# Pooled attention and a tanh-shrink layer on one core: the output product of the last three groups as seven products of quarters

## The chip, the core and the metric

The kernel runs on one core of one Trainium2 chip. The core has five engines, each with its own instruction queue: TensorE (PE in the profile, with its weight loads as PEld), VectorE (DVE), ScalarE (ACT), GpSimd (POOL) and SyncE (SP), which here only issues DMA transfers. TensorE writes its results to PSUM, a memory of eight banks with 512 f32 columns in 128 partitions each; VectorE and ScalarE read them from there into SBUF, GpSimd works on SBUF alone.

The metric is the device time of one execution in microseconds, as the median of several runs.

## What is computed

Pooled attention over 8 batches, 8 heads, 576 queries of 64 elements: keys and values are averaged over 8 neighbouring positions (576 become 72), and each query attends to the 72 pooled positions. The result, 4608 tokens of 512 elements, goes through a layer that widens it to 2048, applies h - tanh(h) and narrows it to 512.

```python
k_p = k.reshape(B, H, Sp, pool, D).mean(axis=3)
v_p = v.reshape(B, H, Sp, pool, D).mean(axis=3)
scores = scale * np.matmul(q, k_p.transpose(0, 1, 3, 2))
scores = scores - np.max(scores, axis=-1, keepdims=True)
attn = np.exp(scores)
attn = attn / (np.sum(attn, axis=-1, keepdims=True) + 1e-09)
attn_out = np.matmul(attn, v_p)                       # 8 x 8 x 576 x 64
x = attn_out.transpose(0, 2, 1, 3).reshape(B * S, H * D)
h = x @ w_in                                          # 4608 x 2048
g = h - np.tanh(h)
out = g @ w_out                                       # 4608 x 512
```

## The kernel before

**Groups.** The 4608 tokens are worked in nine groups of 512. Groups 0 to 7 hold the first 512 tokens of batches 0 to 7, as four blocks of 128; group 8 holds the tails, the last 64 tokens of every batch. Group 0 is written out by hand together with the start of the kernel; groups 1 to 8 run in one loop (`for g in range(1, NG)`, line 706).

**One group** has two phases on TensorE.

- The h phase: 16 steps `i`, each a `h_mms` of four matmuls of 512 columns (line 386) that gives 128 of the 2048 hidden elements in one PSUM bank. After every second step `h_act` works on two banks at once: ScalarE's Tanh into `t_sb` (line 399), then VectorE's subtraction into `gT`, 128 x 1024 in bf16 (line 400). The steps take banks 0 to 5 in turn, so a pair of banks is written again three pairs later.
- The output product: for each of four token blocks `tb`, 16 matmuls of 512 columns (`o_mms`, line 429), four to a unit `u`, 16 units in all. `gT` holds the weights of the array, `w2b` streams through. A finished block is copied by ScalarE to `o_sb` (line 450) and stored by SP (line 453). In group 8 the last block goes through `o_last`: first 384 columns, then 128, each with its copy and its stores.

**The next batch's attention** is laid into the phases of the group before by a table written out by hand, `plan`. Its keys are places: negative ones stand in the h phase (-16 is the first step), the others are units of the output product. Its entries are steps:

- `("s", n)`: the score matmuls of block n (`s_mms`, line 275), then on VectorE the maximum (line 287) and the subtraction (line 290), `s_shift`.
- `("e", n)`: ScalarE's Exp into `E` (line 303).
- `("t", n)`: SP's DMA transpose of two blocks of `E` into `ET` (line 312).
- `("a", n)`: the value matmuls (`av_mms`, line 339), then VectorE's reciprocal and product (`normalise`, lines 360 and 361).
- `("x", n)`: SP's DMA transpose of two normalised blocks into `xT` (line 369), from which the next group's h phase reads.

Block 4 of some batches is the tails' block: two batches' 64 remaining queries together, for group 8. Batch 7 and the last tail's block are worked during group 6. Groups 7 and 8 have nothing of the kind beside them.

**Engines beside.** GpSimd pools values and keys (`pool_v`, lines 208 to 220, and `pool_k`, lines 193 to 199), up to batch 7's values in group 6; ScalarE casts queries (line 244). The order of each engine's queue is the order in which the program is written; an instruction that waits holds up what is behind it on its engine.

Of the kernel before, what the change touches and what calls it, by code (L numbers as in the profile page):

```python
# [28 lines left out]
NK = H * G  # L29
KP = 2 * G  # L30
D1 = D + 1
SCALE = 1.0 / (POOL * float(D) ** 0.5)


@with_exitstack
def kernel(
# [16 lines left out]
    opool = ctx.enter_context(tc.tile_pool(name="opool", bufs=4))  # L53
# [7 lines left out]
    def two(banks, n):  # L61
# [32 lines left out]
    v_sm = const.tile([128, NT, 1, D], FP32, name="v_sm")  # L94
    x_tl = const.tile([128, 1, 2, 4, D], BF16, name="x_tl")
    warm = const.tile([128, 1], FP32, name="warm")
    v_bf = [
        v_raw[i]
        .rearrange("p t n -> p (t n)")
# [1 line left out]
        .rearrange("p (t n) -> p t n", t=NT)  # L101
        for i in range(2)
    ]

    def xT_of(g):
        return xTs[g % 2] if g < B else xTt
# [176 lines left out]
    def s_shift(banks):  # L283
# [8 lines left out]
        )  # L292
        return sh


    def slot(n):
        return E_ps[n // 2 % 2], ET_ps[n // 2 % 2], n % 2
# [129 lines left out]
    def o_mms(tb, i0, i1, bank, c0=0, c1=DM):  # L427
        for i in range(i0, i1):
            nc.tensor.matmul(  # L429
                PS[:, bank, 0 : c1 - c0],  # L430
                lhsT=gT[:, i, tb * 128 : (tb + 1) * 128],
                rhs=w2b[:, i, c0:c1],
                start=(i == 0),
                stop=(i == NHID - 1),
            )
# [10 lines left out]
    stores = []  # L446

    def o_store(g, tb, bank, eng):
        o_sb = opool.tile([128, DM], FP32, name="o_sb", tag="o_sb")
# [6 lines left out]
    def o_last(g, tb, banks):  # L456
        o_sb = opool.tile([128, DM], FP32, name="o_sb", tag="o_sb")
        for n, (c0, c1, eng) in enumerate(
            ((0, 384, nc.scalar.copy), (384, DM, nc.vector.tensor_copy))
        ):  # L460
            o_mms(tb, 0, NHID, banks[n], c0, c1)
            eng(out=o_sb[:, c0:c1], in_=PS[:, banks[n], 0 : c1 - c0])
            for s, (r0, r1, dst) in enumerate(out_rows(g, tb)):
                (nc.sync, nc.scalar)[s].dma_start(out=dst[:, c0:c1], in_=o_sb[r0:r1, c0:c1])

    def fill(n, bank, cols=512):
        for _ in range(n):
# [237 lines left out]
    hn = [0]  # L705
    for g in range(1, NG):
        nb = g + 1 if g + 1 < B else None
        more = nb is not None and nb + 1 < B

        tail = {2: 0, 3: 1, 5: 2, 7: 3}.get(nb)  # L710
        plan = {}
        if nb is not None:
            units = [(s_block(nb, j), av_block(nb), slot(4 * nb + j)) for j in range(4)]
            s_pairs, a_pairs = [0, 0, 0, 1, 2], [0, 1, 0, 2, 1]
            plan = {
                -12: [("s", 0)],
                -9: [("e", 0)],
                -8: [("s", 1)],
                -5: [("e", 1), ("t", 0)],
                -3: [("s", 2)],  # L720
                0: [("e", 2)],
                1: [("s", 3)],
                3: [("e", 3), ("t", 1)],
                4: [("a", 0)],
                5: [("a", 1), ("x", 0)],
                9: [("a", 2), ("a", 3), ("x", 1)],
            }
            if g == 1:
                plan[-10], plan[-7], plan[-5] = plan.pop(-12), plan.pop(-9), plan.pop(-8)
                plan[-2], plan[-1] = [("e", 1), ("t", 0)], plan.pop(-3)  # L730
            if tail is not None:
                units.append((s_tail(tail), av_tail(tail), slot_tl))
                plan[3].append(("s", 4))
                plan[4] += [("e", 4), ("t", 2)]
                if g == 1:
                    plan[6], plan[7] = plan[4][:1], plan.pop(5)
                    plan[4] = plan[4][1:]
                    plan[10] = plan.pop(9)
                plan[12] = [("a", 4), ("x", 2)]
            xs = [x_pair(), x_pair(), x_tl]  # L740
        if nb is not None:
            pool_v(nb, nc.gpsimd)
        shs = {}

        def step(kind, n):
# [9 lines left out]
            if kind == "s":  # L755
                bk = PAIRS[s_pairs[n]]
                s_mms(s, bk)
                shs[n] = s_shift(bk)
            elif kind == "e":
                s_exp(shs[n], sl)  # L760
            else:
                bk = PAIRS[a_pairs[n]]
# [11 lines left out]
        for u, (tb, qd) in enumerate(UNITS):  # L774
            if g == NG - 1 and tb == 3:
                o_last(g, tb, (0, 1))
                break
# [22 lines left out]
_INS = ['q', 'k', 'v', 'moe_w_in', 'moe_w_out']  # L800
# [26 lines left out]
```

## Time and profile before

Three runs: 307.48 us in the median, 306.88 to 308.18. The profiled execution took 306.89 us, of which its span, from the first to the last instruction, is 305.1 us. The mean granted TensorE clock is 0.994 of full speed.

| stage (us from the span's start) | length | TensorE | VectorE | ScalarE | GpSimd | DMA share |
|---|---|---|---|---|---|---|
| group 5, h phase (184.98 to 198.80) | 13.82 | 13.82 | 9.89 | 9.01 | 7.67 | 0.84 |
| group 5, output product (198.80 to 215.03) | 16.23 | 16.12 | 8.62 | 5.77 | 6.23 | 0.86 |
| group 6, h phase (215.03 to 229.43) | 14.40 | 14.40 | 10.47 | 8.90 | 7.60 | 0.46 |
| group 6, output product (229.43 to 246.16) | 16.73 | 16.57 | 10.20 | 4.72 | 0.13 | 0.57 |
| group 7, h phase | 13.81 | 13.81 | 7.81 | 7.76 | 0.00 | 0.08 |
| group 7, output product | 13.82 | 13.71 | 1.98 | 2.78 | 0.00 | 0.16 |
| group 8, h phase (273.79 to 287.60) | 13.81 | 13.81 | 7.82 | 7.76 | 0.00 | 0.05 |
| group 8, output product and end (287.60 to 305.10) | 17.50 | 13.96 | 2.27 | 3.26 | 0.00 | 0.27 |

The table gives busy time in us. TensorE's share is close to the length of each stage, while the other engines have room, most of it in groups 7 and 8; group 6's VectorE has least. A stage of group 6 is longer than one of group 7 by the matmuls of batch 7's attention that stand between the product's own.

Three things help in reading the lines further on. A group's row gives the source line, the engine, the operation, output and inputs with partitions x elements, the count, the busy time and the mean of one, then the engine's idle time before them and what ended it. A row of the timeline gives the start, the length and what ran. Matmuls are pipelined: the record of one is longer than the distance to the next.

### The profile page before, as it was taken

Reading aid. Unit: us, or ns where it says so; the run is one execution under the profiler, and the core shown is the slowest. Engines: PE = TensorE matmul, PEld = TensorE weight load, DVE = VectorE, ACT = ScalarE, POOL = GpSimd, SP = SyncE. Lnnn points to the kernel's source line nnn. Section 1 sums busy time; section 2 is a strip of 40 time slices with the busy share of each in tenths; the row PEclk is TensorE's granted clock in tenths of the full one; section 3 lists DMA queues with packets and bytes.
Section 4 is the critical chain, followed back from the end, with each engine's and each line's share of the span. In section 5 each row is a group of like instructions: output and inputs, shape, how many; then the busy total and the mean of one; then the engine's idle time right before and its main releaser. Section 6 shows DMA issues by size and latency. Waiting matters only on the chain.

```text
span 305.1 us, 4524 instructions
## 1 busy us (share of the span) xinstructions
PE 290.4 (95%) x1734; PEld 150.4 (49%) x1757; DVE 179.4 (59%) x250; ACT 142.3 (47%) x186; POOL 113.5 (37%) x101
## 2 busy tenths in 40 slices
PE   5779989899999999999999999999999999999995
PEld 1457955444554455445544554455445544444443
DVE  4696766458844993398249933983399336305700
ACT  2467756157504751476147613761474136225511
POOL 7544929209610791097109710971080000000000
PEclk9799999999999999999999999999999999999999
DMA  7999997898999998876898799879803830020023
GB/s 232 220 223 309 217 281 164 157 269 288 198 219 213 345 161 183 284 261 123 200 275 280 142 165 282 289 91 219 252 15 73 183 94 0 9 97 34 0 63 77
DMA packets 85894, 54.84 MB, mean 180 GB/s; under 512 B 60368, under 2 KB 73040, under 8 KB 85872
## 3 DMA queue, kind: packets, MB, share of 16 engines
q1 hardware_dynamic: 78192, 44.84, 58.7%
q0 software_dynamic: 6400, 8.91, 14.2%
q10 hardware_dynamic: 1280, 0.79, 0.9%
q8 instruction: 14, 0.23, 0.3%
q14 instruction: 8, 0.07, 0.1%
HBM read 36.70 MB, written 9.44 MB: 151 GB/s over the span
## 4 chain that ended last, share of the span: by engine, by line
PE 84%; DVE 5%; DMA 4%; ACT 4%; issue 1%; ACTq 0%; DVEq 0%
PE PS L429 38%; PE PS L386 35%; PE PS L339 4%; PE PS L275 3%; PE PS L408 2%; DMA k_raw<-in_k_dram 2%; DMA xT<-x_sb 2%; PE PS L256 1%; ACT E L303 1%; DVE sh L290 1%; DVE mx L287 1%; DVE gT L421 1%; DVE x_sb L361 1%; ACT qT L521 1%; ACT t_sb L420 1%
## 5 line engine op out<-in xcount | busy, mean ns | idle before, releaser
L429 PE MATMUL PS<-w2b,gT 128*128 128x512 bf16 (+2 forms) x570 | 131.4, 373 | 1.4 <-ACT v_sm L651 0.2
L400 DVE TENSOR_TENSOR gT<-PS,t_sb 128x1024 bf16<-128x1024 f32 x64 | 77.2, 1220 | 63.4 <-ACT t_sb L399 63.4
L386 PE MATMUL PS<-xT,w1b 128*128 128x512 bf16 x448 | 100.6, 379 | 1.1 <-DMA xT<-x_sb 1.1
L399 ACT ACTIVATE t_sb<-PS 128x1024 f32<-128x1024 f32 x64 | 65.6, 1024 | 44.5 <-PE PS L386 44.5
L429 PEld LDWEIGHTS <-gT 128*128 128x128 bf16 x592 | 54.8, 98 | 58.5 <-issue 0.5
L386 PEld LDWEIGHTS <-w1b 128*128 128x128 bf16 x512 | 49.3, 98 | 58.0 <-issue 2.3
L450 ACT COPY o_sb<-PS 128x512 f32<-128x512 f32 x33 | 19.3, 584 | 73.6 <-PE PS L429 73.6
L208 POOL TENSOR_TENSOR v_raw<-v_raw 128x1280 f32<-128x1280 f32 x6 | 17.4, 2906 | 40.7 <-DMA v_raw<-in_v_dram 40.7
L303 ACT ACTIVATE E<-sh 128x576 bf16<-128x576 f32 x32 | 21.8, 681 | 19.8 <-DVE sh L290 19.8
L287 DVE TENSOR_REDUCE mx<-PS 128x8 f32<-128x576 f32 x36 | 26.9, 748 | 5.6 <-PE PS L275 5.6
L290 DVE TENSOR_TENSOR sh<-PS,mx 128x576 f32<-128x576 f32 x36 | 27.3, 757 | 1.2
L360 DVE RECIPROCAL rden<-PS 128x8 f32<-128x8 f32 x36 | 7.3, 204 | 27.5 <-PE PS L339 27.4
L361 DVE TENSOR_TENSOR x_sb<-PS,rden 128x512 bf16<-128x512 f32 x32 | 22.1, 691 | 1.1
L193 POOL TENSOR_TENSOR k_raw<-k_raw 128x1280 f32<-128x1280 f32 x7 | 20.3, 2905 | 0.1
L244 ACT CAST q_bf<-q_raw 128x1024 bf16<-128x1024 f32 x14 | 14.4, 1038 | 5.5 <-DMA q_raw<-in_q_dram 5.5
L339 PEld LDWEIGHTS <-ET 128*128 128x128 bf16 x192 | 13.1, 98 | 6.1 <-ACT ET L322 0.8
L230 POOL COPY KB<-kT 64x288 bf16<-64x288 bf16 x12 | 5.1, 421 | 29.5 <-DMA kT<-kd 17.8
L408 PE MATMUL PS<-xT,w1b 128*128 128x256 bf16 x128 | 15.3, 273 | 0.7 <-ACT xT L378 0.7
L339 PE MATMUL PS<-VB,ET 128*128 128x130 bf16 (+2 forms) x192 | 15.7, 221 | 0.2 <-ACT ET L322 0.2
L275 PE MATMUL PS<-KB,qT 128*128 128x144 bf16 x128 | 13.1, 226 | 1.3 <-ACT KB L230 0.9
L275 PEld LDWEIGHTS <-qT 128*128 128x128 bf16 x128 | 9.9, 98 | 8.8 <-issue 1.6
L386 PE MATMUL PS<-xTt,w1b 128*128 128x512 bf16 x64 | 14.0, 379 | 0.0
(75 smaller groups left out, 171.7 us busy)
## 6 DMA issues: line engine op xcount, KB each, us to landing
out_dram<-o_sb SPq DMA_DIRECT2D x32, 256.0 KB, 2.7
k_raw<-in_k_dram SPq DMA_DIRECT2D x14, 512.0 KB, 8.4
v_raw<-in_v_dram SPq DMA_DIRECT2D x12, 512.0 KB, 5.0
q_raw<-in_q_dram SPq DMA_DIRECT2D x11, 512.0 KB, 6.8
w1b<-in_moe_w_in_dram POOLq DMA_DIRECT2D x4, 512.0 KB, 9.0
q_raw<-in_q_dram POOLq DMA_DIRECT2D x2, 1024.0 KB, 15.1
w2b<-in_moe_w_out_dram POOLq DMA_DIRECT2D x4, 512.0 KB, 19.2
v_raw<-in_v_dram POOLq DMA_DIRECT2D x2, 512.0 KB, 13.7
```

Source lines behind the costliest of these rows:

```text
L193: eng.tensor_tensor(out=r[:, :, 0:4, :], in0=r[:, :, 0:4, :], in1=r[:, :, 4:8, :], op=ALU.add)
L275: nc.tensor.matmul(PS[ps, banks[m // 2], KP * (m % 2) : KP * (m % 2) + KP], lhsT=qT[:, m, :], rhs=KB[kb][:, m, :], start=True, stop=True,)
L287: nc.vector.reduce_max(out=mx.rearrange("p k h o -> p k (h o)"), in_=sc, axis=AX.X)
L290: nc.vector.tensor_tensor(out=sh[:, :, :, :], in0=sc, in1=mx.to_broadcast([128, 2, 4, G]), op=ALU.subtract)
L303: nc.scalar.activation(out=E[:, e, :, :].rearrange("p t c -> p (t c)")[:, 0:NK], in_=sh.rearrange("p k h c -> p (k h c)"), func=ACT.Exp, s ...
L339: nc.tensor.matmul(PS[ps, banks[half], D1 * h : D1 * (h + s1 - s0)], lhsT=ET[:, t, c0 : c0 + (ps.stop - ps.start)], rhs=VB[kb][:, t, s0:s1 ...
L361: nc.vector.tensor_tensor(out=x_sb, in0=ps[:, :, :, 0:D], in1=rden.to_broadcast([128, 2, 4, D]), op=ALU.mult,)
L386: nc.tensor.matmul(PS[:, bank, :].rearrange("p (j c) -> p j c", j=R), lhsT=w1b[:, fb, i * 128 : (i + 1) * 128], rhs=xT_of(g)[:, :, fb, :], ...
L399: nc.scalar.activation(out=t_sb[:, :, :], in_=ps, func=ACT.Tanh)
L400: nc.vector.tensor_sub(out=gT[:, i : i + 2, :], in0=ps, in1=t_sb[:, :, :])
L408: h_mm_last[0] = nc.tensor.matmul(PS[:, bank, 256 * s : 256 * s + 256].rearrange("p (j c) -> p j c", j=2), lhsT=w1b[:, fb, (2 * n + s) * 1 ...
L429: nc.tensor.matmul(PS[:, bank, 0 : c1 - c0], lhsT=gT[:, i, tb * 128 : (tb + 1) * 128], rhs=w2b[:, i, c0:c1], start=(i == 0), stop=(i == NH ...
```

## The change

**Seven products.** In groups 6, 7 and 8 (`SEVEN`) the output product is taken apart. The 512 x 2048 matrix of a group's `gT` and the 2048 x 512 of `w2b` are cut in halves in both directions, and the product of quarters, which takes eight products of 256 x 1024 by 1024 x 256, is formed from seven, with sums of quarters as their factors (the scheme of Strassen in Winograd's form). Each product has two halves of 128 tokens (`b`), and each of those eight matmuls of 256 columns.

- Four sums of `w2b`, T1 to T4, each in two halves of 128 x 1024 in bf16, are formed once by VectorE in the output product of group 5, one at each unit from 8 on. They lie in the buffers of raw keys and values.
- Four sums of `gT` for each group, S1 to S4, lie in the buffers of raw queries. S3 is formed in two halves (128 x 1024) behind the last two `h_act`, S2 (128 x 2048) at u = 2 and S4 (128 x 2048) at u = 8, all on VectorE; S1 in two halves on GpSimd, behind S2.
- The products run in the order 4, 2, 7, 1, 6, 5, 3. Product 2 has bank 2; the others are added up one after the other in banks 0 and 1, one for each `b`, and each intermediate state that an output needs is copied out before the next product goes on in that bank. In group 6, ScalarE copies and GpSimd forms the differences with earlier states; in groups 7 and 8 VectorE subtracts while it copies.
- Output goes to two fixed tiles `o_h` (`o_hs`), half a group each, in all groups. In groups 6 to 8 it is stored in halves, in group 8 the first half in two pieces of 256 columns.

```diff
+    LO, HI = slice(0, NQ), slice(NQ, NHID)
+    C1, C2 = slice(0, HC), slice(HC, DM)
+    def w_sums():
+        b11, b12, b21, b22 = ((HI, C1), (HI, C2), (LO, C1), (LO, C2))
+        w = lambda q: w2b[:, q[0], q[1]]
+        ops = [
+            (T1, w(b12), w(b11)),
+            (T2, w(b22), T1),
+            (T3, w(b22), w(b12)),
+            (T4, w(b21), T2),
+        ]
...
+    def g_sum(n, i0, i1, eng=nc.vector):
+        i = slice(i0, i1)
+        a11, a12 = gT[:, NQ + i0 : NQ + i1, C1], gT[:, i, C1]
+        a21, a22 = gT[:, NQ + i0 : NQ + i1, C2], gT[:, i, C2]
+        o, x, y, op = {
+            1: (S1, a21, a22, ALU.add),
+            2: (S2, a22, S3[:, i, :], ALU.subtract),
+            3: (S3, a11, a21, ALU.subtract),
+            4: (S4, a12, S2[:, i, :], ALU.subtract),
+        }[n]
+        return eng.tensor_tensor(out=o[:, i, :], in0=x, in1=y, op=op)
+    XB, YB = 2, (0, 1)
+    PRODUCTS = ("4", "2", "7", "1", "6", "5", "3")
+    def product(n, b):
+        A, a0, B_ = {
+            "1": (gT[:, HI, C1], 0, w2b[:, HI, C1]),
+            "2": (gT[:, LO, C1], 0, w2b[:, LO, C1]),
+            "3": (S4, 0, w2b[:, LO, C2]),
+            "4": (gT[:, LO, C2], 0, T4),
+            "5": (S1, 0, T1),
+            "6": (S2, 0, T2),
+            "7": (S3, 0, T3),
+        }[n]
+        ps = PS[:, XB, HC * b : HC * b + HC] if n == "2" else PS[:, YB[b], 0:HC]
+        for i in range(NQ):
+            nc.tensor.matmul(
+                ps,
+                lhsT=A[:, i, 128 * b : 128 * b + 128],
+                rhs=B_[:, i, :],
+                start=(n in "24" and i == 0),
+                stop=(i == NQ - 1),
+                skip_group_check=True,
+            )
+    def evacuate(n, b, plain=False):
+        ps = PS[:, YB[b], 0:HC]
+        if n == "2":
+            if b == 1:
+                nc.scalar.copy(out=p2, in_=PS[:, XB, :].rearrange("p (b c) -> p b c", b=2))
+        elif n in "47":
+            nc.scalar.copy(out={"4": n0, "7": n1}[n][:, b, :], in_=ps)
+        elif n == "6":
+            nc.scalar.copy(out=o_hs[1][:, b, C1], in_=ps)
+        elif plain and n in "15":
+            dst = o_hs[0][:, b, C1] if n == "1" else o_hs[1][:, b, C2]
+            nc.scalar.copy(out=dst, in_=ps)
+        else:
...
+            nc.vector.tensor_sub(out=dst, in0=ps, in1=sub[:, b, :])
...
+        for u in range(14 if g in SEVEN else 0):
+            n, b = PRODUCTS[u // 2], u % 2
+            product(n, b)
+            evacuate(n, b, nb is not None)
+            for it in plan.get(u, ()):
+                step(*it)
+                run_late()
+            if u == 2:
+                dep = g_sum(2, 0, NQ)
+                after([g_sum(1, 0, 4, nc.gpsimd), g_sum(1, 4, NQ, nc.gpsimd)], dep)
+            if u == 8:
+                g_sum(4, 0, NQ)
+            if b == 0:
+                continue
+            if n == "1":
+                finish_11(nc.gpsimd, nb is not None)
+                if g == NG - 1:
+                    store_half(g, 0, C1)
+            elif g == NG - 1 and n == "5":
+                store_half(g, 1)
+            elif g == NG - 1 and n == "3":
+                store_half(g, 0, C2, (nc.sync, nc.scalar))
+            elif n in "53":
+                if n == "5" and nb is not None:
+                    finish_22(nc.gpsimd)
+                store_half(g, 0 if n == "3" else 1)
```

**The order around it.** The h phase of groups 6 to 8 takes its banks in another order, so that the last pair lies in banks 4 and 5. Group 6 has its own plan: all four score blocks of batch 7 stand in the h phase, the fourth (`"sb"`) before the last `h_act`, and the value blocks at u = 3, 5, 6 and 7 of 14. The tail's scores come at u = 9; its value matmuls, their normalisation and their transpose are carried into group 7's h phase, at steps 3 and 5.

```diff
+    HB = ((2, 3), (4, 5), (0, 1))
+    PLAN7 = {
+        -14: [("s", 0)],
+        -11: [("e", 0)],
+        -10: [("s", 1)],
+        -7: [("e", 1), ("t", 0)],
+        -6: [("s", 2)],
+        -3: [("e", 2)],
+        -1: [("sb", 3, P67)],
+        0: [("e", 3), ("t", 1)],
+        3: [("a", 0, P67)],
+        5: [("a", 1, P45), ("x", 0)],
+        6: [("a", 2, P67)],
+        7: [("a", 3, P45), ("x", 1)],
+        9: [("sb", 4, P45)],
+        11: [("e", 4), ("t", 2)],
+    }
...
         for i in range(NHID):
-            h_mms(g, i, i % 6)
+            bk = HB[i // 2 % 3][i % 2] if g in SEVEN else i % 6
+            h_mms(g, i, bk)
+            if g in SEVEN and i == 15:
+                for it in plan.pop(-1, ()):
+                    step(*it)
             if i % 2:
-                h_act(i - 1, (i - 1) % 6)
+                h_act(i - 1, bk - 1)
+                if g in SEVEN:
+                    if i in (3, 5) and carry:
+                        carry.pop(0)()
+                    for n, i0 in {13: [(3, 0)], 15: [(3, 4)]}.get(i, ()):
+                        g_sum(n, i0, i0 + 4)
...
+            if g == SEVEN[0] - 1 and u >= 8 and w_ops:
+                w_ops.pop(0)()
```

More of the change, by code (lines that the diff above doesn't have):

```diff
@@ L96 @@
     warm = const.tile([128, 1], FP32, name="warm")
+    o_hs = [const.tile([128, 2, DM], FP32, name=f"o_h{i}") for i in range(2)]
     v_bf = [
@@ L103, with quarters @@
     ]
+    def quarters(raw):
+        return [
+            raw[:, n * NQ * HC : (n + 1) * NQ * HC].rearrange("p (i c) -> p i c", c=HC)
+            for n in range(2)
+        ]
+    T1, T2 = quarters(k_raw[0].rearrange("p t n -> p (t n)").bitcast(BF16))
+    T3, T4 = quarters(v_raw[0].rearrange("p t n -> p (t n)").bitcast(BF16))
+    S1, S2 = quarters(q_raw[0].rearrange("p h j d -> p (h j d)").bitcast(BF16))
+    S3, S4 = quarters(q_raw[1].rearrange("p h j d -> p (h j d)").bitcast(BF16))
+    p2, n0, n1 = [k_raw[1][:, n, :].rearrange("p (b c) -> p b c", b=2) for n in range(3)]
     def xT_of(g):
@@ L293, in s_shift, with s_max, s_exp_heads @@
         return sh
+    def s_max(banks):
+        sc = two(banks, 4 * G).rearrange("p k (h c) -> p k h c", c=G)
+        mx = work.tile([128, 2, 4, 1], FP32, name="mx", tag="mx")
+        ng = work.tile([128, H], FP32, name="ng", tag="ng", bufs=4)
+        nc.vector.reduce_max(
+            out=mx.rearrange("p k h o -> p k (h o)"), in_=sc, axis=AX.X
+        )
+        nc.vector.tensor_scalar_mul(ng[:, :], mx.rearrange("p k h o -> p (k h o)"), -SCALE)
+        return ng
+    def s_exp_heads(banks, ng, sl):
+        E, ET, e = sl
+        ef = E[:, e, :, :].rearrange("p t c -> p (t c)")
+        for h in range(H):
+            nc.scalar.activation(
+                out=ef[:, G * h : G * h + G],
+                in_=PS[:, banks[h // 4], G * (h % 4) : G * (h % 4) + G],
+                func=ACT.Exp,
+                bias=ng[:, h : h + 1],
+                scale=SCALE,
+            )
     def slot(n):
@@ new lines @@
+    C1, C2 = slice(0, HC), slice(HC, DM)
[7 more added lines that the diff above has]
+            (T4, w(b21), T2),
+        ]
+        return [
+            lambda o=o, x=x, y=y, n=n: nc.vector.tensor_sub(
+                out=o[:, n : n + 4, :], in0=x[:, n : n + 4, :], in1=y[:, n : n + 4, :]
+            )
+            for n in (0, 4)
+            for o, x, y in ops
+        ]
@@ L773 @@
                 q_cast(nb + 1, se, i - 13, i - 11)
[L774 to L777, printed above, removed]
+        for u in range(14 if g in SEVEN else 0):
[24 more added lines that the diff above has]
+                store_half(g, 0 if n == "3" else 1)
+        if g in SEVEN and tail is not None:
+            carry += [lambda i=tail: tail_values(i), lambda i=tail: x_turn_dma(x_tl, B, i, 1)]
+        for u, (tb, qd) in enumerate(() if g in SEVEN else UNITS):
             o_mms(tb, qd * 4, qd * 4 + 4, 4 + tb % 2)
```

68 lines of the change are left out of this document (52 added, 16 removed).

## The prediction

> **What bounds the kernel now.** I read the page's engine rows and its chain of waits first.
>
> ```profile
> span 305.1 us, 4524 instructions
> PE 290.4 (95%) x1734; PEld 150.4 (49%) x1757; DVE 179.4 (59%) x250; ACT 142.3 (47%) x186; POOL 113.5 (37%) x101
> ...
> PE 84%; DVE 5%; DMA 4%; ACT 4%; issue 1%; ACTq 0%; DVEq 0%
> ```
>
> TensorE is busy 95% of the span and carries 84% of the chain. Then the chain in order of time: one line from the start of the kernel for its 256-column matmuls, and the end.
>
> ```profile
> 28.25 7.00 PE PS L408 x64
> ...
> 246.32 13.81 PE PS L386 x64
> ...
> 273.95 13.81 PE PS L386 x64
> ...
> 288.03 13.60 PE PS L429 x78
> 301.63 0.02 issue
> 301.65 0.29 DVE o_sb L462
> ```
>
> In groups 7 and 8 nothing but matmuls is on the path: 64 of 512 columns take 13.81 us (0.2158 each), and 64 of 256 columns 7.00 us (0.1094 each). So a 256-column matmul, with its own weight load, costs half of a 512-column one. Third, busy times by stage: group 6's h phase, then group 7's two phases (columns: stretch, its length, then PE, PEld, DVE, ACT, POOL busy, granted clock, DMA share, GB/s).
>
> ```profile
> 215.03:229.43 14.40, 14.40 (x77) 6.92 (x75) 10.47 (x11) 8.90 (x10) 7.60 (x5) 1.00 0.46 127
> ...
> 246.16:259.97 13.81, 13.81 (x65) 6.24 (x64) 7.81 (x7) 7.76 (x8) 0.00 (x0) 1.00 0.08 25
> 259.97:273.79 13.82, 13.71 (x64) 6.27 (x65) 1.98 (x2) 2.78 (x4) 0.00 (x0) 1.00 0.16 57
> ```
>
> In group 7's product VectorE has under 2 us of work and GpSimd none; in group 6 VectorE is nearly full. Fourth, prices from the groups by form, a pair in the timeline, and the DMA rows.
>
> ```profile
> 222.23 2.34 DVE L400 TENSOR_TENSOR gT<-PS,t_sb 128x1024 bf16<-128x1024 f32 x2
> L400 DVE TENSOR_TENSOR gT<-PS,t_sb 128x1024 bf16<-128x1024 f32 x64 | 77.2, 1220 | 63.4 <-ACT t_sb L399 63.4
> L193 DVE TENSOR_TENSOR k_raw<-k_raw 128x512 f32<-128x512 f32 x2 | 1.4, 688 | 1.3 <-DMA k_raw<-in_k_dram 1.3
> L211 POOL TENSOR_TENSOR v_raw<-v_raw 128x640 f32<-128x640 f32 x6 | 9.3, 1542 | 0.5
> L208 POOL TENSOR_TENSOR v_raw<-v_raw 128x1280 f32<-128x1280 f32 x6 | 17.4, 2906 | 40.7 <-DMA v_raw<-in_v_dram 40.7
> out_dram<-o_sb SPq DMA_DIRECT2D x32, 256.0 KB, 2.7
> out_dram<-o_sb SPq DMA_DIRECT2D x1, 32.0 KB, 1.9
> ```
>
> **The change, part by part.** Below, T is the start of a group's output product, and times run from it.
>
> *Matmuls removed.* Each of three groups has 112 matmuls of 256 columns for 64 of 512: 112 x 0.109 = 12.21 us for 13.81, so 1.60 saved in groups 6 and 7. Group 8's stage ends today at T+14.02 (287.60 to 301.62, its last part in narrower pieces); after, 12.21 + 0.16 (a 256-column record is 0.273 long, 0.109 of it pitch) = 12.37: 1.65. Together 4.85.
>
> *Prices of the sums.* The trace has no bf16 sum between SBUF tiles. For 1024 elements VectorE is bounded by L193's f32 row of the same bytes, 0.69, and L400's row of the same elements, 1.22; for 2048, 1.22 (that 0.69 plus 512 at 1.03 ns, the slope from 425 ns at 256 to 688 at 512) and 2.29. I take the lower: all operands are 16 bits wide and lie side by side, and L193 is the row with both inputs in SBUF. GpSimd: 2906 and 1542 ns give 2.13 ns an element, so 2.36 for 1024; below it is bounded by its one-input rows (421 ns at 288, 610 at 512): 1.04. I take 2.36, the same operation with two dense inputs.
>
> *Groups 7 and 8.* Today the last Tanh runs T+0.20 to 1.22 and the last gT ends at T+2.48. The first half of S3 goes ahead of it on VectorE and delays it to 2.6; S3's second half ends at 3.3, S2 at 4.6. Product k of 14 starts at 0.872k. Product 7 (k=4) needs the second half of S3 at 3.92: 0.6 to spare. Product 6 (k=8, 6.98) has S2 in time. S1 follows S2 on GpSimd: 4.63 to 7.0 and 7.06 to 9.43. Product 5 (k=10) needs its second half at 9.16: a wait of 0.33 in each group, 0 with the cheap GpSimd sum. S4 comes after the copies of product 1 (7.6) and is ready at 8.8, needed at 10.46. A bank is emptied in 0.63 to 0.69 (0.2 to start, 0.37 on ScalarE or 0.43 on VectorE, 0.06 back) while the other takes 0.87. ScalarE has six such copies and one of 512 columns (0.58), 2.8 us of 12, and in group 6 ten, one and two exps, 5.6 of 14. SP issues two stores a group in place of four. The tail's value matmuls (12, 0.65 us) only move from group 6 to 7; VectorE's 0.9 there falls into idle time, and the transpose behind it on SP has some 20 us until group 8.
>
> *Group 6* (from its first h matmul). Score block 3 moves into the h phase, so T comes at 13.81 + 4 x 0.25 = 14.81. VectorE's queue starts at 3.03, as today (217.90 less 214.87), and holds eight gT at 1.13 (two back to back: 2.34 less one's 1.22, so the next starts 0.09 before the last ends), four score pairs at 1.46 (0.78 + 0.68 between starts), 0.64 and 0.72 for S3: 3.03 + 9.04 + 5.84 + 1.36 = 19.27. The second half of S3 is needed at 14.81 + 3.92 + 0.36 (block 0's value matmuls) = 19.09. With 0.06 to signal, product 7 waits some 0.3. Blocks 2 and 3: their last exp ends at 18.2, the transpose behind it on SP lands 3.6 later (median of 14; 2.9 to 5.0), at 21.8; the value matmuls that need it stand at 21.9. That is 0 by the median, 1.4 by the slowest. x for group 7: the last transpose goes out near 24.7 and lands at 28.0 (4.8 at the slowest: 29.5), needed at 29.1. The halves' stores wait on SP for GpSimd, which finishes near 30.7; what stands behind them is the tail's transpose, not urgent.
>
> *The eight weight sums in group 5.* Seven fall into VectorE's idle 6.60 us before group 6's first gT: 7 x 0.61 = 4.3, hidden. At 1.22 each they take 8.0 and start group 6 about 1.4 late on its tightest engine. Loads and scores they share VectorE with are done.
>
> *The end.* SP issues at about 0.53 a transfer. Group 8's first quarter store waits for GpSimd's last addition (9.43 + 1.28 = 10.8), two issues; the half behind it goes out at 11.86 and 12.4, the last quarter at 13.16 (12.37 + 0.04 + 0.43, signals). From 32 KB in 1.9 to 256 KB in 2.7 a store costs 1.8 us plus 280 KB per us, so 768 KB from 11.86 land at 11.86 + 1.8 + 2.74 = T+16.40. Today the last lands at 302.0 + 2.1 = 304.1, T+16.5. The saving of group 8 itself is thus lost in the stores: they cost 0.5 to 1.9 us (free flow, last quarter at 13.16 + 2.4 = 15.56; 220 KB per us, 17.1), and I take 16.4.
>
> *Sum.* T of group 8 moves by 1.60 + 1.60 - 0.30 - 0.33 = 2.57 to 285.03; the last landing is 301.4 for 304.1: 2.7 less. Against the profiled execution's own 306.89 us (span 305.1 plus 1.8 around it) that is 304.2. It lies 0.6 under the median of 307.48, and on the median's scale the forecast is 304.8.
>
> **Rivals.**
> *Cheap GpSimd sums* (2.0 or less). For: two of its rows run at less per element (L220, 960 in 1.80). Against: taking off the 0.18 that the two-input rows leave at no elements, its bf16 copy (421 ns at 288) and its cast from f32 (610 at 512) both cost 0.84 ns an element, so width seems not to matter. No wait in 7 and 8, and the half's store leaves at 11.15: 287.60 - 2.90 + 11.15 + 4.55 = 300.4, or -3.7: 303.8.
> *GpSimd and VectorE exclude each other on two-input sums.* Then S4 waits for S1's end (9.43), ends at 10.7, and the copies of product 5 and GpSimd's last addition come after it; product 3 starts 0.25 late, the first store leaves at 12.0 and the half at 13.1. 287.60 - 2.32 + 13.1 + 4.55 = 302.9: -1.2, 306.3. Against it: L208's 2906 ns stay within 2897 to 2914 whatever VectorE does beside them. But VectorE has an input in PSUM there each time, so the case itself is not in the trace. The Trainium skill says it outright ("SBUF — State Buffer", Who interferes with whom): a VectorE instruction with two SBUF inputs contends with a GpSimd one that reads SBUF, and the second is held until the first ends; by it the time is this rival's.
> *VectorE sums at a cycle per element*, the other side. Against it: L193's row is the only one with both inputs in SBUF, but it is f32, and L400's writes bf16 at 1.22, which speaks for it. Prices: group 6 waits 1.4 for S3 and 0.7 for VectorE's late normalisations; groups 7 and 8 wait 0.53 for S3 (ends at 4.4) and 1.95 for S1 (behind S2, until 11.5). PE ends at -4.85 + 2.1 + 2 x 2.48 = +2.2, and the stores' 1.2 stay: +3.4, 310.9. It decides from some 0.95 us for 1024 elements, where these waits have eaten the gain. The Trainium skill ("VectorE: DVE Perf Modes", The perf-mode tier table) gives 1224 ns for 2048 bf16 elements in SBUF, which would leave my sum as it is and speaks against this rival.
> *Late transpose in group 6*, 1.4 us by the slowest of the 14: 306.2.
>
> **How the numbers follow.** Forecast 0.42, cheap GpSimd 0.20, exclusion 0.19, full-rate VectorE 0.13, late transpose 0.06. The time is the likeliest's, 304.8. The range from 303.0 (below the second case, with the stores flowing freely) to 307.6 (above the third and fourth) leaves out the +3.4 and little else. About 0.5% (1.5 us) is what a measurement can tell here from no change. Faster than 305.9: 0.40 + 0.20 + 0.07 of the third and fourth = 0.67; within: 0.20; slower: 0.13, the full-rate case.
>
> **What would show it.** Matmuls of 256 columns at a pitch of 0.109 in the three stages, and 12.2 us for a stage plus its waits; VectorE's sums at 0.69 and 1.22; GpSimd's near 2.36; a wait of 0.3 in product 5; S4 starting at 7.6, not at 9.4; the last stores landing 4.5 us after the half's issue. It would be wrong if the sums ran at a cycle per element, or if GpSimd's took well over 2.4 beside VectorE.

## The result, and the profile after

The changed kernel takes 306.26 us in the median (20 runs, 305.55 to 307.75) against 307.36 for the kernel before (20 runs, 306.88 to 308.44). The ratio is 0.9962, with a 95% interval of 0.995 to 0.9974: 1.1 us less, where the forecast was 2.7. The profiled execution took 306.24 us, its span 304.2.

In the new code the matmuls of the h phase are line 425, those of the product 545 and those of the old product 468; the sums of `gT` are line 527, the copies with a subtraction 572, the last addition of the first quarter (`finish_11`) 578, and the stores of group 8 line 593. First the busy times by stage (columns as before): group 6's two phases, group 7's two, group 8's two, and what follows TensorE's last matmul.

```profile
215.52:230.33 14.81, 14.81 (x81) 7.25 (x80) 12.45 (x15) 9.47 (x11) 7.59 (x5) 1.00 0.61 142
230.33:244.91 14.58, 14.46 (x147) 12.40 (x145) 12.29 (x19) 6.50 (x14) 8.72 (x6) 1.00 0.39 65
244.91:259.49 14.58, 14.58 (x78) 6.74 (x78) 9.05 (x10) 7.17 (x7) 0.32 (x1) 1.00 0.28 92
259.49:271.71 12.22, 12.22 (x113) 10.96 (x112) 8.71 (x11) 3.74 (x8) 6.41 (x3) 1.00 0.03 9
271.71:285.53 13.82, 13.82 (x67) 6.27 (x65) 8.24 (x8) 7.17 (x7) 0.00 (x0) 1.00 0.18 71
285.53:297.93 12.40, 12.39 (x113) 10.86 (x111) 8.68 (x11) 3.73 (x8) 6.41 (x3) 1.00 0.00 0
297.93:304.20 6.27, 0.00 (x0) 0.00 (x0) 0.42 (x1) 0.00 (x0) 0.00 (x0) 0.82 0.67 167
```

The last two rows of the kernel before, for group 8's product and what follows it, and its first stores:

```profile
287.60:301.62 14.02, 13.96 (x80) 7.15 (x79) 1.98 (x2) 3.26 (x5) 0.00 (x0) 1.00 0.26 57
301.62:305.10 3.48, 0.00 (x0) 0.00 (x0) 0.29 (x1) 0.00 (x0) 0.00 (x0) 1.00 0.30 78
```

```profile
293.59 6.29 SPq L453 DMA_DIRECT2D out_dram<-o_sb  x6
```

The products of groups 7 and 8 have shrunk from 13.82 and 14.02 to 12.22 and 12.40 us, with no gap on TensorE. From the start of group 6 to TensorE's last matmul it was 86.75 us (214.87 to 301.62) and is 82.41: 4.34 less. But the last row has grown: after TensorE's last matmul the kernel went on for 3.48 us before and goes on for 6.27 now, 2.79 more. And in the row above it nothing was moved by DMA: 0 GB/s during the whole of group 8's product, where the kernel before issued its first store 5.99 us into it. From the start of group 6 the changed kernel is thus 1.55 us shorter, while the two spans differ by 0.9. The other 0.65 us is the start of group 6, 215.52 for 214.87. It is there at group 1 already (60.97 for 60.20), and two kernels below that are the same up to group 8 started group 6 at 214.70 and 216.28; so I put it down to the execution.

The chain of waits shows where group 6 is bound now and how the rest runs (start, length, engine, line, count).

```profile
230.94 0.60 DVE q_raw L527
...
232.99 1.14 DVE gT L439
...
234.16 0.70 DVE q_raw L527
...
259.65 12.23 PE PS L545 x112
271.88 13.81 PE PS L425 x64
285.69 12.24 PE PS L545 x112
297.93 0.02 issue
297.96 0.42 DVE o_h L572
```

Group 6's path runs through VectorE's queue, whose last piece is the second half of S3, which product 7 waits for. Groups 7 and 8 are matmuls alone. The chain stops at the last copy, at 298.4, because nothing that it can follow comes later: what is left is DMA. The two views of SP after 293 (what it waited for, and its issues) and the DMA engines in 40 slices of 0.325 us from 293 to 306 show it.

```profile
SPq L593 <- POOL o_h L578: 23.8, 1, 23.8
```

```profile
296.61 3.56 SPq L593 DMA_DIRECT2D out_dram<-o_h  x5
298.41 0.71 ACTq L593 DMA_DIRECT2D out_dram<-o_h  x1
```

```profile
DMA  0000000000000005878889979998850000000020
GB/s 0 0 0 0 0 0 0 0 0 0 0 0 0 0 0 145 199 196 189 205 189 202 183 177 315 296 262 246 230 183 13 0 0 0 0 0 0 0 50 0
```

SP stood 23.8 us for GpSimd's last addition and issued its first store at 296.61, which is 11.08 us into the product. Data moved from 297.9 to 302.9, so all 1,024 KB of group 8 went out behind TensorE's last matmul, at some 190 GB/s for most of the time. The DMA engines were 80 to 90% busy at that rate, so they were not short of work.

### The profile page after: what moved, and what is told of

It is laid out like the page before. It is cut to its first block, busy times and chain, and to the rows that moved or that the text cites. A ratio compares the mean times of both kernels' runs of the same rounds, so it can differ in the third digit from the quotient of the medians.

```text
span 304.2 us, 4875 instructions
## 1 busy us (share of the span) xinstructions
PE 287.7 (95%) x1885; PEld 164.0 (54%) x1885; DVE 202.8 (67%) x283; ACT 145.0 (48%) x199; POOL 135.4 (45%) x112
## 4 chain that ended last, share of the span: by engine, by line
PE 80%; DVE 10%; DMA 3%; ACT 3%; issue 1%; ACTq 0%; DVEq 0%
PE PS L425 31%; PE PS L468 26%; PE PS L545 11%; PE PS L378 4%; DVE gT L439 3%; PE PS L447 3%; PE PS L291 3%; DMA k_raw<-in_k_dram 2%; DVE sh L306 2%; DVE mx L303 2%; PE PS L272 2%; DMA xT<-x_sb 1%; PE PS L599 1%; DVE x_sb L400 1%; ACT E L342 1%
## 5 line engine op out<-in xcount | busy, mean ns | idle before, releaser
L468 PE MATMUL PS<-w2b,gT 128*128 128x512 bf16 x384 | 89.8, 379 | 0.2 <-ACT v_sm L782 0.2
L438 ACT ACTIVATE t_sb<-PS 128x1024 f32<-128x1024 f32 x64 | 65.6, 1024 | 49.8 <-PE PS L425 48.4
L468 PEld LDWEIGHTS <-gT 128*128 128x128 bf16 x384 | 35.3, 98 | 37.7 <-issue 0.5
L489 ACT COPY o_h<-PS 128x512 f32<-128x512 f32 x22 | 12.8, 584 | 45.9 <-PE PS L468 45.8
L527 POOL TENSOR_TENSOR q_raw<-gT 128x1024 bf16<-128x1024 bf16 x6 | 12.6, 2122 | 44.3 <-PE PS L545 38.5
L545 PEld LDWEIGHTS <-q_raw 128*128 128x128 bf16 x192 | 18.5, 98 | 2.6 <-DVE q_raw L527 0.4
L378 PE MATMUL PS<-VB,ET 128*128 128x130 bf16 (+2 forms) x192 | 15.8, 221 | 0.2 <-ACT ET L361 0.2
L545 PEld LDWEIGHTS <-gT 128*128 128x128 bf16 x144 | 13.9, 98 | 2.0
```

Of the source, the lines that this page charges most:

```text
L378: nc.tensor.matmul(PS[ps, banks[half], D1 * h : D1 * (h + s1 - s0)], lhsT=ET[:, t, c0 : c0 + (ps.stop - ps.start)], rhs=VB[kb][:, t, s0:s1 ...
L438: nc.scalar.activation(out=t_sb[:, :, :], in_=ps, func=ACT.Tanh)
L468: nc.tensor.matmul(PS[:, bank, 0 : c1 - c0], lhsT=gT[:, i, tb * 128 : (tb + 1) * 128], rhs=w2b[:, i, c0:c1], start=(i == 0), stop=(i == NH ...
L545: nc.tensor.matmul(ps, lhsT=A[:, i, 128 * b : 128 * b + 128], rhs=B_[:, i, :], start=(n in "24" and i == 0), stop=(i == NQ - 1), skip_grou ...
```

## The experiments

The miss lies in the end. What had to be told apart was whether group 8's product as such costs the time, whether the late start of the stores does (and the addition that they wait for), or the rate at which they go. The experiments were run in two sets, each beside the kernel before; the changed kernel's row is that of the result above, a set of its own. Times "after TensorE" are from each kernel's one profiled execution. They carry some scatter (the end stays 1.3 to 2.1 us behind the last packet, and the profiled executions of the early stores, of S1 on VectorE and of the early stores on two queues were the longest of their six), so the verdicts rest on the medians. Between kernels of different sets a difference of medians is less sure: the kernel before itself took 307.37 in one of the two and 307.61 in the other.

| kernel | median, us | ratio to before, 95% interval | first store, us into group 8's product | after TensorE, us |
|---|---|---|---|---|
| before | 307.37 and 307.61 | | 5.99 (old product) | 3.48 |
| changed | 306.26 | 0.9962 (0.995 to 0.9974) | 11.08 | 6.27 |
| groups 6 and 7 only | 305.55 | 0.9926 (0.99 to 0.9952) | old product | 4.62 |
| group 8 only | 308.82 | 1.0041 (1.0022 to 1.006) | 11.04 | 6.44 |
| early stores | 304.32 | 0.9889 (0.9861 to 0.9917) | 8.43 | 5.33 |
| S1 on VectorE | 304.86 | 0.9906 (0.988 to 0.9933) | 9.96 | 6.12 |
| two queues | 305.01 | 0.9931 (0.9908 to 0.9954) | 11.07 | 5.62 |
| early stores, two queues | 303.61 | 0.9881 (0.986 to 0.9903) | 8.43 | 3.99 |
| group 8 only, mended stores | 306.10 | 0.9952 (0.9935 to 0.9968) | 8.42 | 3.73 |

### Groups 6 and 7 only

```diff
-SEVEN = (6, 7, 8)
+SEVEN = (6, 7)
...
+            if g == NG - 1 and tb == 3:
+                o_last(g, tb, (0, 1))
+                break
```

> The new product in groups 6 and 7 only; group 8 uses the old product of 64 matmuls of 512 columns and its old stores, four blocks of which three leave while TensorE still works. Theory A (the miss is in the end: in the changed kernel no store of group 8 leaves before GpSimd's last addition, 11 us into the stage, and 1 MB goes out after that): TensorE's end comes 1.6 us later than in the changed kernel (12.4 us of group 8 become 14.0), but the time after TensorE's end falls from 6.3 to 3.5 us: in sum 1.1 to 1.2 less than the changed kernel, 305.0 to 305.2 against 306.3, and 2.2 to 2.4 less than the kernel before. Rival B (the new product of groups 6 and 7 is worth less than forecast, or group 6 starts later through the weight sums, and group 8 gave its full 1.6): then this kernel is 1.6 slower than the changed one, near 307.9. Rival C (the hold between GpSimd's sums and VectorE's sums costs matmul time in group 7 too): group 7's stage is well over 12.4 us here.

It is 1.8 us faster than before and 0.7 faster than the changed kernel: with less of the change the kernel gains more. Rival B falls, since it needed a slower kernel than the changed one. Rival C falls with this row of the stages, group 7's product, as long as in the changed kernel:

```profile
258.71:270.94 12.23, 12.23 (x114) 10.96 (x113) 8.71 (x11) 3.74 (x8) 6.41 (x3) 1.00 0.03 9
```

The gain is 0.4 less than expected. The end was 4.62 us here where the same stores took 3.48 in the kernel before; the last 32 KB landed later behind their issue (3.0 us by the rows of DMA issues), and why is not known.

### Group 8 only

```diff
-SEVEN = (6, 7, 8)
+SEVEN = (8,)
```

> The new product in group 8 only; groups 6 and 7 as in the kernel before (batch 7's score blocks back in the products, eight weight sums still made, now in group 7). Theory A: TensorE gains 1.6 in group 8 and the end after it grows by 2.8, so the kernel is 1.1 to 1.2 slower than the one before (about 308.5). Rival B: group 8's saving counts, 1.6 faster than before (305.8). A fall between the two, near 307.4, would say that group 8's part is worth nothing, as the forecast had it (last landing at T+16.4 for T+16.5).

1.45 us slower than before, and the interval lies above 1. The last two rows of the stages are those of the changed kernel again:

```profile
288.09:300.49 12.40, 12.39 (x113) 10.86 (x111) 8.67 (x11) 3.74 (x8) 6.41 (x3) 1.00 0.01 2
300.49:306.93 6.44, 0.00 (x0) 0.00 (x0) 0.43 (x1) 0.00 (x0) 0.00 (x0) 0.79 0.65 162
```

TensorE's 1.6 us are gained and 2.96 are lost behind it. So group 8's part of the change does not merely fail to pay, as the forecast had it. It costs 1.45 us alone, and beside groups 6 and 7 it takes back part of what they gain: 0.7 us by the medians, 1.1 by the ratios.

### Early stores

```diff
-            if n == "1":
+            if n == "1" and g == NG - 1:
+                o = o_hs[0][:, :, C1]
+                x2 = PS[:, XB, :].rearrange("p (b c) -> p b c", b=2)
+                nc.vector.tensor_tensor(out=o, in0=o, in1=x2, op=ALU.add)
+                store_half(g, 0, C1)
+            elif n == "1":
                 finish_11(nc.gpsimd, nb is not None)
-                if g == NG - 1:
-                    store_half(g, 0, C1)
+            elif g == NG - 1 and n == "6":
+                store_half(g, 1, C1)
             elif g == NG - 1 and n == "5":
-                store_half(g, 1)
+                store_half(g, 1, C2)
```

> The changed kernel with group 8's stores taken apart: VectorE, not GpSimd, makes the last addition of the first quarter, from PSUM, and that quarter (256 KB) is stored right after, about 8 us into the stage; of the second half one quarter is stored after product 6 and one after product 5; the last quarter as it was. Bytes, transfers' shapes and TensorE's work are the same but for two more transfers. Theory A (start of the stores): 512 KB are out before TensorE ends, the time after TensorE's end falls from 6.3 to about 4.0 to 4.5: 1.8 to 2.3 less than the changed kernel, 304.0 to 304.5. Rival D (these transfers of 64 partitions are slow wherever they stand, and the last quarter alone needs the time): the last landing stays 5 us behind TensorE's end, under 0.7 gained. Rival C (the hold of S4 behind GpSimd's sums delays the matmuls): S4 is still 2.3 long here, so nothing is gained.

304.32 us, 1.9 less than the changed kernel: theory A, at the size expected. SP's first issue is at 294.85, with TensorE's last matmul ending at 298.82. The profiled execution took 305.86, so its 5.33 after TensorE, where 4.0 to 4.5 was expected, is not what the median has. It shows the second half of the matter, though: with SP the only queue at work, the rate stays where it was, however early the stores start (DMA in slices of 0.125 us from 296 to 301):

```profile
GB/s 0 74 197 213 188 197 156 230 156 246 147 197 172 205 213 180 205 172 222 238 172 188 188 172 229 147 246 139 222 221 205 188 197 148 25 0 74 328 188 164
```

Rival D has the rate of these transfers right, but their start counts all the same. Rival C expected S4 to be 2.3 us long and nothing to be gained. S4 came later here and took 1.60 us, and TensorE's stage is 12.40 us as before. VectorE's addition in front of it, with one input in PSUM, ran beside GpSimd's S1 (291.06 to 295.26) in 0.69 us:

```profile
291.06 4.20 POOL L527 TENSOR_TENSOR q_raw<-gT 128x1024 bf16<-128x1024 bf16 x2 [19.66 <-PE PS L545]
294.14 0.69 DVE L968 TENSOR_TENSOR o_h<-o_h,PS 128x512 f32<-128x512 f32 x1
294.74 1.60 DVE L527 TENSOR_TENSOR q_raw<-gT,q_raw 128x2048 bf16<-128x2048 bf16 x1
```

### S1 on VectorE

```diff
-                after([g_sum(1, 0, 4, nc.gpsimd), g_sum(1, 4, NQ, nc.gpsimd)], dep)
+                if g == SEVEN[0]:
+                    after([g_sum(1, 0, 4, nc.gpsimd), g_sum(1, 4, NQ, nc.gpsimd)], dep)
+                else:
+                    g_sum(1, 0, NQ)
```

> The changed kernel with the sum S1 of groups 7 and 8 made by VectorE in one instruction behind S2 (GpSimd keeps it in group 6); GpSimd's last addition stays, and so do all stores. Theory A: VectorE has room (S1 1.2 us, at 4.6 to 5.9 of the stage, needed at 8.7); S4 and the addition no longer stand behind GpSimd's S1, the addition ends some 2 us earlier (1.3 to 2.3 long, from 7.7 of the stage), the first quarter's stores leave at 9.5 to 10 in place of 11.1; the second half still waits for its copies at 11.1. The end shrinks by 0.8 to 1.3: 305.0 to 305.5. If the hold between the two engines were without a part in the end (only the number of bytes behind TensorE's last product counts), the time stays at 306.3. If S1 on VectorE made TensorE wait, group 7's product would grow over 12.4 and the time over 306.3.

304.86 us, 1.4 less than the changed kernel, a little more than expected. What it takes away is seen in the timelines of VectorE and GpSimd. The changed kernel first, with S2, S1, S4 and the addition in group 8 (start, length, engine, line):

```profile
288.78 1.22 DVE L527 TENSOR_TENSOR q_raw<-gT,q_raw 128x2048 bf16<-128x2048 bf16 x1
290.17 4.20 POOL L527 TENSOR_TENSOR q_raw<-gT 128x1024 bf16<-128x1024 bf16 x2 [19.66 <-PE PS L545]
293.13 2.33 DVE L527 TENSOR_TENSOR q_raw<-gT,q_raw 128x2048 bf16<-128x2048 bf16 x1
294.32 2.26 POOL L578 TENSOR_TENSOR o_h<-o_h,k_raw 128x512 f32<-128x512 f32 x1
```

The same addition in group 6 of this kernel, with no sum of VectorE from two SBUF inputs beside it:

```profile
242.73 1.27 POOL L578 TENSOR_TENSOR o_h<-o_h,k_raw 128x512 f32<-128x512 f32 x1
```

Then S1 and S4 in group 8, and the addition in groups 7 and 8, with S1 on VectorE:

```profile
289.88 1.22 DVE L527 TENSOR_TENSOR q_raw<-gT 128x2048 bf16<-128x2048 bf16 x1
293.08 1.22 DVE L527 TENSOR_TENSOR q_raw<-gT,q_raw 128x2048 bf16<-128x2048 bf16 x1
```

```profile
267.26 2.12 POOL L578 TENSOR_TENSOR o_h<-o_h,k_raw 128x512 f32<-128x512 f32 x1 [22.34 <-DVE o_h L572]
293.25 2.18 POOL L578 TENSOR_TENSOR o_h<-o_h,k_raw 128x512 f32<-128x512 f32 x1 [23.86 <-DVE o_h L572]
```

S4 takes 1.22 us when GpSimd is idle and 2.33 when it starts at 293.13 beside S1, which ends at 294.37: 294.37 less 293.13 is 1.24, and the 1.09 that is left is close to its own length. So VectorE's sum of two SBUF inputs waited for GpSimd's. Next the addition, started at 294.32, ends at 296.58. Its own work, 1.27 us as in group 6, would begin at 295.31, about the end of S4 (295.46). It waited in its turn, and in the second kernel it waits for S4 again (2.18). The recorded length includes the wait. In the changed kernel the two holds put the first store 1.0 us later than S1's end allows: 294.37 and 1.27 give 295.64, and SP issued at 296.61.

The profile of this kernel shows less than its median (6.12 after TensorE for 6.27, where the medians differ by 1.4). In that execution, which took 305.72, one issue of SP took 1.5 us, where the others take 0.6 to 0.75, and what stood behind it was late.

### Two queues

```diff
                 if g == NG - 1:
-                    store_half(g, 0, C1)
+                    store_part(g, 0, C1, 0, nc.sync)
+            elif g == NG - 1 and n == "6":
+                store_part(g, 0, C1, 1, nc.scalar)
             elif g == NG - 1 and n == "5":
-                store_half(g, 1)
+                store_half(g, 1, engs=(nc.sync, nc.scalar))
```

Here `store_part` is one of the two transfers of `store_half`: the fourth argument 0 is partitions 0 to 63, 1 is 64 to 127.

> The changed kernel; each store of group 8 is two transfers of 64 partitions, and here the second of each pair (partitions 64 to 127) goes out on ScalarE's queue in place of SP's, for the first quarter behind product 6's copies. Sums, order of products and bytes as in the changed kernel. Theory P (ports: a transfer of 64 partitions alone gets half the rate, and on one queue the transfers go one after another): in the changed kernel a packet of 1 KB takes 73 ns and one of 2 KB 153 ns while one queue is at work, 46 and 84 ns when two are, and group 7's 4 KB packets from 128 partitions 141 ns. So with both halves in flight the 1 MB takes 2.6 to 3.5 us in place of 4.9: last landing at about 15.8 to 16.4 of the stage in place of 17.7, and 1.2 to 1.9 less than the changed kernel: 304.4 to 305.1. Rival Q (small packets of 1 KB, or the memory's side, set the rate): about 200 GB/s with two queues as well, under 0.4 gained beyond the saved issue time of SP (each issue 0.6 to 0.75).

305.01 us: 1.25 less than the changed kernel in the medians, at the low edge of what theory P expected. The two kernels come from different sets, though. By the ratios to the kernel before the gain is 0.95, with intervals that touch, and in the profiled executions the time after TensorE falls by 0.65. The last store landed at 17.0 of the stage (issued at 298.06, 4.1 us to land, less 285.18), 0.7 earlier than in the changed kernel, where theory P expected 15.8 to 16.4. So the direction is right, and the size is smaller than expected. Rival Q falls by the rate: in the best half microsecond it doubles. First the DMA of the changed kernel from 297.9 to 299.3, where packets of 1 KB go out on SP's queue alone, and from 299.3 to 300.6, where they are of 2 KB (header, packets, queue; the share is of 16 engines' time):

```profile
DMA packets 271, 0.26 MB, mean 184 GB/s; under 512 B 20, under 2 KB 271, under 8 KB 271
...
q1 hardware_dynamic: 271, 0.26, 79.0%
```

```profile
DMA packets 136, 0.25 MB, mean 191 GB/s; under 512 B 12, under 2 KB 17, under 8 KB 136
...
q1 hardware_dynamic: 136, 0.25, 93.4%
```

Packets twice as long go no faster, 191 for 184 GB/s, so their size is not it. Now the kernel with two queues, from 298.5 to 299:

```profile
DMA packets 149, 0.20 MB, mean 395 GB/s; under 512 B 16, under 2 KB 89, under 8 KB 149
...
q1 hardware_dynamic: 60, 0.12, 65.4%
q10 hardware_dynamic: 89, 0.07, 46.5%
```

395 GB/s, with packets of the same two sizes on the same 16 engines. The changed kernel's own group 7 stores from 128 partitions in one transfer, and its slices show the same rate on SP's queue alone (from 271.5 to 275, 0.0875 us each):

```profile
GB/s 515 374 421 421 374 374 374 515 281 515 374 421 468 374 94 0 0 0 0 187 421 374 421 421 374 374 374 468 328 515 468 374 374 421 94 0 0 0 0 0
```

Those packets are of 4 KB. A closer pair stands in the kernel before, both with packets of 2 KB on SP's queue alone: a store of group 7 from 128 partitions (271.9 to 272.6), and stores of group 8 from 64 (294.8 to 296).

```profile
DMA packets 111, 0.24 MB, mean 345 GB/s; under 512 B 0, under 2 KB 0, under 8 KB 110
```

```profile
DMA packets 139, 0.25 MB, mean 208 GB/s; under 512 B 17, under 2 KB 17, under 8 KB 139
```

So a transfer that reads 64 partitions goes at about half the rate of one that reads 128, 184 to 208 GB/s for 345 and more. (Their rows lie differently in DRAM too, and no run takes that apart.) On one queue the rate stays there although the next transfer has been issued; with two queues it reached that of 128 partitions for a time. That the two have to read different halves is not shown. From 301 to 301.75 in the changed kernel, ScalarE's queue and, by the order of its stores, SP's both read partitions 64 to 127, and the rate was above 190 there too:

```profile
DMA packets 142, 0.22 MB, mean 290 GB/s; under 512 B 11, under 2 KB 61, under 8 KB 142
```

The Trainium skill says outright that 64 partitions are slower ("SBUF — State Buffer", Door 1: The DMA port swizzle): partitions 0 to 63 reach 8 of 16 ports, and it measured 196 GB/s for them against 328 for 128 partitions; the trace agrees with 184 to 208. Its rule that two transfers to disjoint halves serialize ("DMA: Bandwidth & Descriptors", Rules for kernel authors) fits one queue, and not two, where 395 was measured for half a microsecond and the whole end moved its bytes in 4.2 us for 4.9.

The whole of the end did not run at 395 (DMA of this kernel in slices of 0.1125 us from 297.5 to 302):

```profile
GB/s 46 191 173 191 155 173 173 237 373 364 373 410 455 328 273 200 146 182 146 273 346 291 373 300 255 300 255 228 255 264 282 291 319 228 182 119 100 73 0 0
```

Both queues issued their first transfer at 296.25, yet until 298.2 only SP's packets moved, at 154 GB/s from 297.5 on. Why ScalarE's came later is not shown. In all, 1,024 KB took 4.2 us (297.6 to 301.8) for 4.9.

### Early stores on two queues, and the last quarter by block

```diff
+            if g == NG - 1 and n == "3":
+                store_part(g, 0, C2, 0, nc.sync, b)
+                store_part(g, 0, C2, 1, nc.scalar, b)
+                continue
```

with the stores of the two kernels above otherwise, each pair on both queues.

> The early stores of the earlier run (first quarter added on VectorE and stored at 8.4 of the stage, the second half in two quarters), each pair of transfers on SP's and ScalarE's queues, and the last quarter cut in two blocks, the first of them stored while the last product's second block is computed. If the end is the start of the stores and their rate alone, only 128 KB are left after TensorE's end and land 2.0 to 2.4 us after their issue (64 KB took 2.1 in the kernel before): the time after TensorE's end falls from 6.3 to 3.5 to 3.9, 2.4 to 2.8 less than the changed kernel: 303.5 to 303.9, and 0.4 to 0.8 less than with early stores alone. If a floor of some 4.5 us lies after TensorE whatever is stored, it stays at 304.3.

303.61 us, the lowest median: 2.65 less than the changed kernel, and 4.0 less than the one before (3.0 to 4.3 by the interval). Against early stores alone it is 0.7 less by the medians, as expected, but the ratios (0.9881 and 0.9889) do not tell the two apart. The floor of 4.5 us behind TensorE is not there; the profiled execution (304.78) has 3.99 after it. The last two pieces are issued 0.5 us behind TensorE's end, after their copy, and 64 KB land 2.1 and 2.3 us after their issue:

```profile
out_dram<-o_h SPq DMA_DIRECT2D x2, 64.0 KB, 2.1
out_dram<-o_h ACTq DMA_DIRECT2D x2, 64.0 KB, 2.3
```

### Group 8 only, with the mended stores

The kernel above with `SEVEN = (8,)`.

> The new product in group 8 alone, with the mended stores of the run before it. With the plain stores group 8 alone cost 1.4 more than the kernel before. If only the stores stood against it, TensorE's 1.6 now show: time after TensorE's end 3.5 to 3.9 against 3.5 in the kernel before, so 1.2 to 1.6 less than before: 305.8 to 306.2. If group 8's product costs something else (the sums' hold, the weight sums' place in group 7), it stays above 307.

306.10 us, 1.5 less than before, where the same product with the plain stores was 1.45 slower. So what stands between the product and the landing (the last addition, the start of the stores and their queues, which this run changes together) decides whether group 8's seven products gain 1.5 us or lose as much.

```profile
287.81:300.22 12.41, 12.39 (x113) 10.86 (x111) 8.64 (x12) 3.74 (x8) 4.20 (x2) 1.00 0.17 45
300.22:303.95 3.73, 0.00 (x0) 0.00 (x0) 0.42 (x1) 0.00 (x0) 0.00 (x0) 0.89 0.51 140
```

## Why the prediction was right in its direction and wrong in size

- **Matmuls.** Right. The products of groups 7 and 8 are 1.60 and 1.62 us shorter; 1.60 and 1.65 were forecast.
- **Prices on VectorE.** Right: 0.687 us for 1024 elements and 1.22 for 2048, so the rival of a cycle per element is out.
- **GpSimd's price.** Taken too high: the two halves of S1 take 4.20 us, 2.12 each, where two-input f32 rows gave 2.36. At 2.12 the waits of 0.33 us of product 5 do not occur, as in the rival of cheap sums.
- **Group 6.** Its h phase is 14.81 us, as forecast. Product 7 waited 0.40 for S3, where 0.3 was forecast (the forecast's own terms, 19.27, 0.06 and 19.09, give 0.24). Group 7's start waited 0.3 for `xT`, which the forecast had 1.1 us early. The late transpose of block 2 did not show.
- **Weight sums.** Hidden, as forecast: from group 1's to group 6's start it is 154.55 us after and 154.67 before.
- **Start of group 8's product.** From group 6's start it comes 2.72 us earlier (70.01 for 72.73); 2.57 was forecast. That these are so close is partly luck, since the waits in group 6 and at group 7's start were longer than forecast and those of product 5 did not come.
- **The end.** This is the step that failed. The forecast lets the second half leave at 11.86 and 12.4, calls the 768 KB from there 1.8 us plus 280 KB per us, and lands at 16.4; it landed at 17.7 (the last 128 KB, issued at 299.42, took 3.8 us: 303.2 less 285.53). The terms, each from the changed kernel's rows: the addition let the first store go at 11.08 in place of 10.8; SP needed 0.73 us for each of the first quarter's two issues (296.61, 297.34, 298.07) in place of 0.53, which makes 0.4; and the 768 KB landed 5.16 us after the half's first issue, at 12.54, in place of 4.54, which is 0.62. Together 1.3 us. The forecast took its rate, 280 KB per us, from a row of 32 KB and one of 256 KB, and the 256 KB transfers read 128 partitions each, while those of group 8 read 64. The kernel before had the row that fits, its own stores of group 8 from 64 partitions: 128 KB in 2.4 us, which with 32 KB in 1.9 gives 192 KB per us (row `out_dram<-o_sb SPq DMA_DIRECT2D x6, 128.0 KB, 2.4`). The last quarter was ready in time: ScalarE issued its part at 12.88, where the forecast had 13.16 (its terms 12.37, 0.04 and 0.43 give 12.84); SP's part stood behind the half until 13.89. Of the 1.6 us between the forecast and the medians, the later landing explains 1.3, less 0.15 that TensorE came earlier; the rest, some 0.45, lies between the profiled executions and the medians, and is not explained.
- **The exclusion.** It was a rival with a chance of 0.19, and its time, 306.3, is the one measured, but only half by its own steps. The hold is there, and without it the cheaper S1 would have let the first store go at about 10.1. But product 3 did not wait, and the first store left at 11.08, not 12.0; S1 had ended at 8.84 and not at 9.43. The rest of that time came from the rate of the stores. The Trainium skill's rule ("SBUF — State Buffer", Who interferes with whom) is what this trace shows, 1.1 us for S4 and 1.0 for the addition. The forecast's argument against it, that GpSimd's rows did not vary, rested on pairs in which VectorE read PSUM, as it said itself, and did not bear on the case.

Either of the two faults alone, mended, brings the median close to the forecast of 304.8 (304.86 without the hold, 305.01 with two queues), though the second is less sure than the first, as said above. The early start alone goes beyond it, to 304.32, and with two queues the median is 303.61.

## What to carry to other kernels

A faster last stage is worth only what its last results let through: ask when the first byte of the stage can be stored, and how many bytes are left when the bounding engine stops. Price a store by a row that reads as many partitions as it does; here 64 went at about half the rate of 128. If such transfers must stand at the end, issue them early first, and then try them on two queues. Where GpSimd and VectorE both add from SBUF, let one of them read PSUM, or give one of them all of the work.

## What the runs showed of the hardware that had not been expected

- A sum on VectorE with two SBUF inputs and one on GpSimd do not run beside each other. The one that came later was held for about 1 us, in both directions, and its record includes the wait (S4 2.33 us for 1.22; the addition 2.18 and 2.26 for 1.27). A VectorE sum with one input in PSUM was not held (0.69 us beside S1).
- One 64-partition store at a time moved 184 to 191 GB/s, with packets of 1 KB as with those of 2 KB, at 79 and 93% busy DMA engines; two on two queues moved 395 in their best half microsecond, and all of the end 1,024 KB in 4.2 us for 4.9. A busy DMA engine is no sign that the rate is at its peak.
- GpSimd's sum of two bf16 inputs, 1024 elements, takes 2.12 us, less than the 2.36 that its f32 rows give.
